# A feed-forward stage behind a recurrent attention stage: transfers put in another order at the hand-over, next input tiles loaded one by one between weight chunks, small transfers held to another stage

## The chip, the cores and the metric

One core of one Trainium2 chip. The metric is the device time of one execution in microseconds (us). One execution with a profile gives the trace that the readings below come from.

Engines: PE is TensorE's matmuls, PEld its weight loads, DVE is VectorE, ACT is ScalarE, POOL is GpSimd, SP is SyncE. SP issues nearly all loads here, on one hardware queue. GpSimd issues the small ones, on a software queue.

## The reference, cut to what matters

```python
g = _sigmoid((x * gate_w).sum(-1, keepdims=True))
a = _A_ref(x, A_mem0, A_Wq, A_Wk, A_Wv, A_Wo, A_seg_len)     # 64 segments, one after the other
b = _gelu(x @ w_gate) * (x @ w_up) @ w_down                  # x: 2048 x 1024, F = 3584, bf16
return g * a + (1 - g) * b
```

The kernel computes `a` segment by segment for about 1670 us. Then it computes `b`, the FFN, in four blocks of 512 rows, and mixes `a` and `b` at the end of each. The change touches only the FFN and the loads in front of it.

## The kernel before

A block is a gate/up stage of 28 groups (each is 8 matmuls with a gate chunk and 8 with an up chunk, 128x512), then a w_down stage of two passes. Gate and up weights stay in SBUF after block 0. w_down does not fit: each pass streams it again in 7 chunks of 1 MB through three buffers.

```python
early = [load_xo, lambda: load_xT(0), lambda: load_w(0), lambda: load_w(1), lambda: load_w(2)]
...                                    # issued by SP in this order at the end of the last segment
def load_xT(fb):                       # the x tiles of a block: four tiles of 256 KB, one transfer of 1 MB
    op("sp", lambda e: e.dma_start(xT[...], xq_scr[TB * fb:TB * fb + TB]...), wr=[xT.r()], lane="xt")
...
for fb in range(NFB):                                  # 4 blocks
    for j in range(NJ):                                # gate/up: 28 groups
        if fb == 0 and j == sum(CH[:2]):
            last_tail()                                # output matmuls of the last 4 segments; reads xo
        ...                                            # 16 matmuls, gelu and product on ACT and DVE
        if todo and j % 3 == 2:
            mix(*todo.pop(0))                          # DVE: g*a + (1-g)*b; then GpSimd stores the tile
        if j in ((8, 16) if fb == 0 else (0, 14)):
            for tb in ...: load_a(fb * TB + tb)        # GpSimd: two loads of a, 256 KB each
    for ps in range(NPS):                              # w_down: 2 passes
        for c in range(NWD):                           # 7 chunks of 1 MB
            if ps == NPS - 1 and c == 1 and not lastb:
                load_xT(fb + 1)                        # next x tiles, 1 MB
            ...                                        # 16 matmuls; todo: mix of the pass before
            load_wd()                                  # chunk c + 3, when PE is done with chunk c
        todo += [...]                                  # 4 mixes of this pass's two tiles
```

`xo` are three tiles of 512 KB of output weights. They are used only after the seventh gate/up group.

## Time and profile before

| | |
|---|---|
| time, 4 runs | 2296.72 us median (2293.88 to 2299.78) |
| profiled run | 2290.79 us, span 2288.8 us |
| FFN: last matmul of the segments to end of span | 1673.28 to 2288.8, 615.5 us |
| one w_down chunk: 16 matmuls of 0.216 us | 3.45 us |

The page of the kernel before: busy time and share of each engine.

```profile
PE 2090.5 (91%) x36642; PEld 1103.0 (48%) x36642; DVE 913.0 (40%) x2166; ACT 604.9 (26%) x1280; POOL 616.1 (27%) x1137
```

PE is busy 91% of the span, so a change has to remove what is left of PE's idle time. The waits of PE from 1600 us to the end, kernel before. Columns: the waiting instruction and its line, what it waited for, us in total, times, longest.

```profile
PE pb L1005 <- DMA wd<-in_B_w_down_dram: 10.5, 3, 3.7
PE pb L948 <- DMA wg<-in_B_w_gate_dram: 9.5, 1, 9.5
...
PE pb L719 <- DVE GT L964: 1.8, 1, 1.8
```

L1005 are the w_down matmuls, L948 the gate/up matmuls, L719 the output matmuls of the last segments. The next lines are from the timeline of PE, kernel before. Columns: start, duration, line, output<-inputs, shapes, count, and in brackets the idle time in front and what ended it.

```profile
1672.87 0.40 PE L689 MATMUL pb<-sl,oT 128*32 128x256 bf16 x8 [0.46 <-DMA sl<-in_A_Wo_dram]
1682.81 3.57 PE L948 MATMUL pb<-xT,wg 128*128 128x512 bf16 x8 [9.53 <-DMA wg<-in_B_w_gate_dram]
1686.17 2.15 PE L948 MATMUL pb<-xT,wu 128*128 128x512 bf16 x8
...
1828.51 10.53 PE L1005 MATMUL pb<-wd,GT 128*128 128x512 bf16 x48 [3.34 <-DMA wd<-in_B_w_down_dram]
...
1977.16 12.04 PE L1005 MATMUL pb<-wd,GT 128*128 128x512 bf16 x48 [3.44 <-DMA wd<-in_B_w_down_dram]
...
2127.62 11.90 PE L1005 MATMUL pb<-wd,GT 128*128 128x512 bf16 x48 [3.75 <-DMA wd<-in_B_w_down_dram]
```

There is one wait of 9.5 us at the hand-over, and one of 3.3 to 3.8 us in each of the first three w_down stages. Eight gate matmuls take 1.89 us in a steady stretch, but 3.57 us after the hand-over. The 48 matmuls after the first stall take 10.53 us, after the second and third 12.04 and 11.90. The table of stretches tells why: its third column from the right, PEclk, is the clock that PE was granted, as a share of the full clock.

```profile
core 0: us, PE busy (x) PEld busy (x) DVE busy (x) ACT busy (x) POOL busy (x), PEclk, DMA share, GB/s
...
1977.20:1980.60 3.40, 3.40 (x9) 1.25 (x10) 0.00 (x0) 0.00 (x0) 0.00 (x0) 0.55 1.06 389
2127.60:2131.00 3.40, 3.38 (x10) 1.29 (x11) 0.00 (x0) 0.00 (x0) 0.00 (x0) 0.58 1.05 386
1828.50:1832.00 3.50, 3.49 (x17) 1.61 (x18) 0.00 (x0) 0.00 (x0) 0.00 (x0) 1.00 1.05 387
```

So a stall can cost more than its length: after two of the three the clock was near half for some 3.4 us. DMA ran at about 387 GB/s, full. What was in the queue then? SP's own timeline, kernel before (start, us, queue, line, what it issues, count):

```profile
1665.68 3.96 SPq L571 DMA_DIRECT2D xo<-in_A_Wo_dram  x3
1669.69 0.47 SPq L529 DMA_DIRECT2D xT<-xq_scr  x1
1670.20 0.51 SPq L536 DMA_DIRECT2D wg<-in_B_w_gate_dram  x1
...
1815.25 0.51 SPq L529 DMA_DIRECT2D xT<-xq_scr  x1
1818.29 145.47 SPq L548 DMA_DIRECT2D wd<-in_B_w_down_dram  x14
```

At the hand-over the three xo stand ahead of what PE needs first. In the second pass of w_down the x tiles (1 MB, 1815.25) stand ahead of the chunk issued at 1818.29, and PE starts on that chunk at 1828.51, 10.2 us later. With three buffers a chunk has the computing of two others, 6.9 us, between its issue and its use. GpSimd's timeline shows what else ran then:

```profile
1814.54 0.54 POOL L934 DMA_DIRECT2D out_dram<-osb  x1 [94.67 <-DVE osb L928]
1817.30 0.55 POOL L934 DMA_DIRECT2D out_dram<-osb  x1 [2.21 <-DVE osb L928]
1817.83 1.07 POOL L554 DMA_DIRECT2D asb<-a_scr  x2
```

That is two stores and two loads of 256 KB each, 1 MB more.

### The profile page before, as it was taken

How to read it: one execution, taken by the hardware profiler on the slowest of the kernel's cores; microseconds unless marked ns; L12 is line 12 of the kernel's file. 1: busy time of each engine (PE TensorE's matmuls, PEld its weight loads, DVE VectorE, ACT ScalarE, POOL GpSimd, SP SyncE). 2: the span in 40 equal slices, each digit the busy share in tenths (PEclk: the TensorE clock that was granted, in tenths of full speed). 3: DMA queues.
4: the chain of work that ended last, by engine and by line, in shares of the span. 5: the costliest groups of instructions: out<-in, count | busy, mean ns of one | idle time of the engine just before them, and what ended most of it. 6: DMA issues, size and time to landing. Idle time of an engine off the chain costs nothing.

```text
span 2288.8 us, 80092 instructions
## 1 busy us (share of the span) xinstructions
PE 2090.5 (91%) x36642; PEld 1103.0 (48%) x36642; DVE 913.0 (40%) x2166; ACT 604.9 (26%) x1280; POOL 616.1 (27%) x1137
## 2 busy tenths in 40 slices
PE   2589999999999999999998999998879999999999
PEld 1244555555555555555555455554434444444444
DVE  3234343344343343343343343343335255263462
ACT  1122232232322233232232322222223033031230
POOL 5233333333332433423333333433210000000000
PEclk9899999999999999999999999999999999999999
DMA  9968788788788787787887887887784620704622
GB/s 349 396 208 301 270 302 290 270 300 305 268 310 292 264 321 280 265 321 277 284 318 262 282 312 268 296 312 265 262 311 154 225 87 27 268 19 143 211 88 92
DMA packets 224224, 576.43 MB, mean 252 GB/s; under 512 B 30472, under 2 KB 43272, under 8 KB 223888
## 3 DMA queue, kind: packets, MB, share of 16 engines
q1 hardware_dynamic: 190256, 513.88, 62.8%
q0 software_dynamic: 29024, 52.01, 7.3%
q8 instruction: 287, 4.70, 0.8%
q10 hardware_dynamic: 4608, 5.44, 0.7%
q14 instruction: 49, 0.40, 0.0%
HBM read 539.71 MB, written 31.39 MB: 250 GB/s over the span
## 4 chain that ended last, share of the span: by engine, by line
PE 78%; DMA 12%; issue 4%; POOL 3%; DVE 1%; ACT 1%; SPq 0%; DVEq 0%; POOLq 0%; ACTq 0%
PE pb L677 26%; PE pb L948 17%; PE pb L689 9%; PE pb L704 7%; PE pb L1005 7%; DMA sl<-in_A_Wo_dram 4%; PE pb L589 4%; PE pb L719 3%; DMA sl<-in_A_Wv_dram 3%; PE pb L610 2%; DMA wd<-in_B_w_down_dram 1%; DMA a_scr<-a_bf 1%; PE pb L604 1%; PE pb L987 1%; PE pb L643 1%
## 5 line engine op out<-in xcount | busy, mean ns | idle before, releaser
L677 PE MATMUL pb<-sl,hT 128*32 128x512 bf16 x12288 | 749.7, 383 | 22.7 <-issue 9.7
L677 PEld LDWEIGHTS pb<-sl,hT 128*32 128x32 bf16 x12288 | 332.7, 97 | 291.1 <-issue 24.9
L689 PE MATMUL pb<-sl,oT 128*32 128x256 bf16 x8192 | 282.5, 275 | 43.7 <-issue 36.4
L577 ACT ACTIVATE tok<-pb 128x512 bf16<-128x512 f32 x320 | 191.0, 597 | 428.9 <-PE pb L677 368.8
L662 POOL COPY oRc<-oT 128x128 bf16<-128x128 bf16 x128 | 97.4, 761 | 637.2 <-DVE oT L580 614.2
L689 PEld LDWEIGHTS pb<-sl,oT 128*32 128x32 bf16 x8192 | 207.7, 97 | 94.2 <-issue 47.3
L704 PE MATMUL pb<-sl,hR 128*32 128x512 bf16 x3072 | 233.8, 395 | 18.4 <-DMA sl<-in_A_Wq_dram 8.2
L948 PE MATMUL pb<-xT,wg 128*128 128x512 bf16 x896 | 213.4, 381 | 9.5 <-DMA wg<-in_B_w_gate_dram 9.5
L948 PE MATMUL pb<-xT,wu 128*128 128x512 bf16 x896 | 211.9, 379 | 0.0
L1005 PE MATMUL pb<-wd,GT 128*128 128x512 bf16 x784 | 173.3, 383 | 10.5 <-DMA wd<-in_B_w_down_dram 10.5
L580 DVE CAST oT<-pb 128x160 bf16<-128x160 f32 x256 | 71.0, 319 | 211.1 <-PE pb L653 210.7
L956 ACT ACTIVATE s<-pb 128x512 f32<-128x512 f32 x112 | 66.9, 597 | 327.1 <-PE pb L948 327.1
L934 POOL DMA_DIRECT2D out_dram<-osb x14 | 7.6, 546 | 533.0 <-DVE osb L928 533.0
L577 ACT ACTIVATE vA<-pb 128x512 bf16<-128x512 f32 x128 | 76.4, 597 | 262.6 <-PE pb L677 262.6
L948 PEld LDWEIGHTS pb<-xT,wg 128*128 128x128 bf16 x896 | 87.9, 98 | 116.1 <-issue 11.6
L580 DVE COPY kT<-pb 128x512 bf16<-128x512 bf16 x128 | 51.9, 405 | 230.1 <-PE pb L589 92.2
L948 PEld LDWEIGHTS pb<-xT,wu 128*128 128x128 bf16 x896 | 87.8, 98 | 106.2 <-issue 0.8
L589 PE MATMUL pb<-ident,tok 128*128 128x128 bf16 x1280 | 127.8, 222 | 12.0 <-ACT tok L577 3.9
L957 DVE SCALAR_TENSOR_TENSOR tp<-s,pb 128x512 f32<-128x512 f32 x112 | 76.9, 686 | 153.9 <-ACT s L956 153.6
L589 PEld LDWEIGHTS pb<-ident,tok 128*128 128x128 bf16 x1280 | 72.9, 98 | 123.4 <-ACT tok L577 92.9
L1005 PEld LDWEIGHTS pb<-wd,GT 128*128 128x128 bf16 x784 | 77.2, 99 | 106.0 <-DMA wd<-in_B_w_down_dram 12.0
L615 DVE TENSOR_REDUCE st<-pb 128x8 f32<-128x320 f32 x128 | 62.9, 491 | 146.1 <-PE pb L610 146.1
(80 smaller groups left out, 2056.8 us busy)
## 6 DMA issues: line engine op xcount, KB each, us to landing
sl<-in_A_Wv_dram SPq DMA_DIRECT2D x394, 512.0 KB, 8.8
sl<-in_A_Wo_dram SPq DMA_DIRECT2D x205, 512.0 KB, 6.0
sl<-in_A_Wk_dram SPq DMA_DIRECT2D x142, 512.0 KB, 5.6
wd<-in_B_w_down_dram SPq DMA_DIRECT2D x49, 1024.0 KB, 5.3
sl<-in_A_Wq_dram SPq DMA_DIRECT2D x79, 512.0 KB, 7.2
qk_scr<-stg POOLq DMA_DIRECT2D x64, 128.0 KB, 6.0
qkr<-qk_scr POOLq DMA_DIRECT2D x128, 64.0 KB, 2.3
wl<-in_B_w_down_dram SPq DMA_DIRECT2D x7, 1024.0 KB, 7.8
```

Of the source, the lines that this page charges most:

```text
L577: op("act", lambda e: e.activation(o, i, ACTF.Copy), rd=rd, wr=wr)
L580: op("dve", lambda e: e.tensor_copy(o, i), rd=rd, wr=wr)
L589: ins = e.transpose(PBV[TT][:, j * 128:(j + 1) * 128], tok[:, j * 128:(j + 1) * 128], ident[:, :])
L662: op("pool", lambda e: e.tensor_copy(oRc[:, u, :, :].rearrange("p c x -> p x c"), oT[:, :, :, 32:40].rearrange("p g j c -> p (g j) c")), r ...
L677: ins = e.matmul(PB[bk][32 * g:32 * g + 32, :], lhsT=h[:, i, :], rhs=w[:, g * 512:(g + 1) * 512], start=(p % 8 == 0), stop=(p % 8 == 7))
L689: ins = e.matmul(PB[XO][32 * g:32 * g + 32, 0:256], lhsT=oT[:, gp_, 2 * jj + hh, 0:32], rhs=w[:, c:c + 256], start=(r == 0 and p % 8 == 0 ...
L704: ins = e.matmul(PB[b][32 * g:32 * g + 32, :], lhsT=h[:, k[2], :], rhs=w[:, g * 512:(g + 1) * 512], start=(n == 0), stop=(n == 7))
L719: ins = e.matmul(PB[b][32 * g:32 * g + 32, 0:256], lhsT=t[:, :, 2 * i + hh], rhs=w[:, c:c + 256], start=(ends[0] and i == 0 and hh == 0), ...
L948: ins = e.matmul(PB[bk][:, 0:FB], lhsT=w[:, kc, cc:cc + 128], rhs=xT[:, :, :, kc, :].rearrange("p t i c -> p (t i) c"), start=(kc == 0), s ...
L956: op("act", lambda e, hg=hg: e.activation(s1[:, :], hg, ACTF.Square, scale=SQ), rd=[BK(bg)], wr=[s1.r()])
L957: op("dve", lambda e, hg=hg, t=t: e.scalar_tensor_tensor(out=t[:, :], in0=s1[:, :], scalar=1.0, in1=hg, op0=ALU.add, op1=ALU.mult), rd=[BK ...
L1005: ins = e.matmul(PB[bank[2 * k + hf]][:, :], lhsT=GT[:, j, tb * 128:(tb + 1) * 128], rhs=w[:, jj, hf * 512:(hf + 1) * 512], start=(j == 0) ...
```

## The change

Three things: (1) at the hand-over, x tiles and gate/up chunks 0 and 1 are issued before xo; (2) the next x tiles are loaded one by one, between the w_down chunks 1 to 4 of the second pass; (3) the small transfers of GpSimd, the stores of the first pass and the loads of a, are held until PE has done a group of the next gate/up stage, where DMA has little to do.

```diff
-        early = [load_xo, lambda: load_xT(0), lambda: load_w(0), lambda: load_w(1), lambda: load_w(2)]
+        early = [lambda: load_xT(0), lambda: load_w(0), lambda: load_w(1), load_xo, lambda: load_w(2)]
...
-        def load_xT(fb):
+        def load_xT(fb, t0=0, n=TB):                    # n of the tiles; one lane (semaphore) per t0
...
-                    if ps == NPS - 1 and c == 1 and not lastb:
-                        load_xT(fb + 1)
+                    if ps == NPS - 1 and 1 <= c <= TB and not lastb:
+                        load_xT(fb + 1, c - 1, 1)
...
+                while held:                             # in the gate/up loop, after group j = 0
+                    put(held.pop(0), 0, D, after=[pe_j])
...
-                if j in ((8, 16) if fb == 0 else (0, 14)):
+                if j in (8, 16):
                     for tb in range(2 * (j > 8), min(TB, 2 * (j > 8) + 2)):
-                        load_a(fb * TB + tb)
+                        load_a(fb * TB + tb, [pe_j])
...
-                todo += [(fb * TB + tb, 512 * hf, 512, bank[2 * k + hf]) for k, tb in enumerate(tbs) for hf in range(2)]
+                todo += [(fb * TB + tb, 512 * hf, 512, bank[2 * k + hf], "late" if ps < NPS - 1 and not lastb else "pool")
+                         for k, tb in enumerate(tbs) for hf in range(2)]
```

More of the change, by code (lines that the diff above doesn't have):

```diff
@@ L526, in bass_gated_mix__memory_aug_recurrent_mem_tr__geglu_ffn__prompt_kernel @@
         osb = [al2(f"osb{t}", [128, D]) for t in range(2)]
-        def load_xT(fb):
-            op("sp", lambda e: e.dma_start(xT[:, :, :, :, :].rearrange("p t i k c -> p t (i k c)"),
-                                           xq_scr[TB * fb:TB * fb + TB].rearrange("t p i c -> p t (i c)")),
-               rd=[("D", "xq", T) for T in range(TB * fb, TB * fb + TB)], wr=[xT.r()], lane="xt")
+        def load_xT(fb, t0=0, n=TB):
+            tn = 4 * KC * SEG
+            op("sp", lambda e: e.dma_start(xT[:, t0:t0 + n, :, :, :].rearrange("p t i k c -> p t (i k c)"),
+                                           xq_scr[TB * fb + t0:TB * fb + t0 + n].rearrange("t p i c -> p t (i c)")),
+               rd=[("D", "xq", T) for T in range(TB * fb + t0, TB * fb + t0 + n)], wr=[xT.r(t0 * tn, (t0 + n) * tn)], lane=f"xt{t0}")
         def load_w(c):
@@ L550, in load_wd, with load_a @@
                wr=[wd[n % 3].r()], lane=f"wd{n % 3}")
-        def load_a(T):
+        def load_a(T, after=()):
             t = asb[T % 4]
@@ L555, in load_a @@
                rd=[("D", "a", s) for s in range(4 * T, 4 * T + 4)] + [("D", "ar", T, g) for g in range(4)], wr=[t.r()],
-               lane=f"al{T % 4}")
+               lane=f"al{T % 4}", after=after)
         tail = slots[home["o", 0, 0]].off
@@ L930, in mix, with put @@
                rd=[BK(b), d.r(), gal.r()], wr=[ob.r(c0, c0 + n)])
-            if eng == "pool" and c0 == 0:
+            if eng != "sp" and c0 == 0:
+                return
+            if eng == "late":
+                held.append(T)
                 return
             c1 = c0 if eng == "sp" else 0
-            op(eng, lambda e: e.dma_start(of[T * 128:(T + 1) * 128, c1:c0 + n], ob[:, c1:c0 + n]),
-               rd=[ob.r(c1, c0 + n)], wr=[("D", "out", T, c0)], lane=f"out{T % 2}" if eng == "pool" else f"oute{c0}")
+            put(T, c1, c0 + n - c1, eng)
+        def put(T, c1, n, eng="pool", after=()):
+            ob = osb[T % 2]
+            op(eng, lambda e: e.dma_start(of[T * 128:(T + 1) * 128, c1:c1 + n], ob[:, c1:c1 + n]),
+               rd=[ob.r(c1, c1 + n)], wr=[("D", "out", T, c1)], lane=f"out{T % 2}" if eng == "pool" else f"oute{c1}", after=after)
+        held = []
         todo = []
@@ L951, in f @@
                         return ins
-                    op("pe", f, rd=[w.r(), xT.r()], wr=[BK(bk)])
+                    pe_j = op("pe", f, rd=[w.r(), xT.r()], wr=[BK(bk)])
+                while held:
+                    put(held.pop(0), 0, D, after=[pe_j])
                 hg, hu = PB[bg][:, 0:FB], PB[bu][:, 0:FB]
```

## The prediction

> **What bounds the kernel now.** TensorE: on the page PE is busy 2090.5 of 2288.8 us (91%) and holds 78% of the chain of waits. The change touches only the FFN (from 1673 us). There PE computes nearly without gaps, so its idle times count. PE's waits from 1600 us show two kinds that the change aims at.
>
> 1. Hand-over: 9.5 us idle (1673.3 to 1682.8) until gate chunk 0 lands. DMA is saturated (about 380 GB/s in the slices from 1660 to 1700), so its order decides. SP issues three xo loads (512 KB each) from 1665.7, x tiles (1 MB) at 1669.7, gate chunk 0 at 1670.2, landing 12.5 us later. xo is read only at 1710.8.
>
> 2. One stall in each w_down stage but the last: 3.3, 3.4, 3.8 us, at the fifth chunk of the second pass. A chunk (1 MB) is consumed in 16 matmuls, 3.45 us; with three buffers it has 6.9 us from issue to use. Median landing is 5.3 us. There 1 MB of x tiles sits ahead in the queue, and two 256 KB stores and two 256 KB loads of a (GpSimd timeline: 1814.5 to 1818.9) share the engines: the chunk took 10.2 us. After the second and third stalls the granted clock was 0.60 and 0.58 for some 4 us. Those blocks take 150.2 and 150.3 us, against 145.1 worked out from 0.216 us a matmul (672): 5.1 and 5.2 lost. Block 0 loses 3.5 in w_down.
>
> **What the change does.** No compute is added. x tiles and gate/up chunks 0 and 1 go before xo: 1.5 MB less ahead of gate chunk 0, about 4.1 us at 385 GB/s. The instruction order shows no new wait before the x tiles. The next x tiles become four 256 KB loads, one per w_down chunk; the stores of pass 0 and the loads of a move into the next gate/up stage, where DMA is nearly idle. A step of the second pass then moves 1.25 MB per 3.45 us, about 380 GB/s, for four steps: near saturation (380 to 410), but without backlog, so a chunk should land in 5.5 to 6.5 us, inside 6.9. Nine more DMA issues on SP are hidden.
>
> The Trainium skill ("DMA: Bandwidth & Descriptors", Queues, rings and completion order) says each DMA engine takes turns between queues per packet, so GpSimd's transfers delay SP's; the 10.2 us agrees. "TensorE: Matmul & The Clock Gate", Part 1, says an idle array's clock is halved until about 3.4 us of work; 0.58 and 0.60 agree, but after the first stall the clock was 1.00.
>
> **On the critical path:** all of it, PE being what each stage waits on. Hand-over -4.1; its slow first matmuls (clock 0.50, about 1.8 us lost) stay, as about 5.4 us of idling remain. Stalls with clock loss: -3.5 -5.1 -5.2 = -13.8. Sum -17.9: about 2279 us, 0.8% faster, within 2%.
>
> **What would show it.** PE's waits: about 5.4 us on gate chunk 0, none on w_down (10.5 before). Gate/up starts 145 to 146 us apart. w_down landings in the second pass at most 6.9 us. First-pass stores after the next block's first gate/up group, loads of a after groups 8 and 16; VectorE's mix at group 2 not waiting for the held stores. The 32 segments and last block unchanged.
>
> **What would make it wrong.** A 256 KB x load still pushing a chunk past 6.9 us (stalls of 1 to 3 us remain per block); the last segment's Wo loads landing later; up chunk 1 arriving just after need (margin about 1 us); a shorter idle leaving the clock full (1.8 us more gain); segments shifting by a few us.
>
> Range 2274 to 2287. Chances: faster by over 2% 0.01, within 2% 0.98, slower 0.01.

## More of the kernel before

The executions of this program differ among themselves by over 1% (the kernel before: 2281.96 to 2309.39 us over all batches), so a difference of 2 us cannot be read from the times. It can be read from the trace, stage by stage, and most of this document does that.

## The result, and the profile after

The changed kernel takes 2277.2 us in the median (2271.78 to 2279.16, 4 runs) against 2296.72; the ratio is 0.9911, with a 95% interval of 0.9888 to 0.9934. A ratio here is the mean time of one kernel's runs over that of the other's of the same rounds, so it is not quite the ratio of the medians. In two later batches it came to 0.9905 and 0.9933. So the kernel is 15 to 22 us faster, 0.7 to 1.0%, which is within 2%. The results are correct.

The line numbers moved a little: L948 became L958, L1005 became L1017, L719 became L720. PE's waits from 1600 us, changed kernel:

```profile
PE pb L958 <- DMA wg<-in_B_w_gate_dram: 4.3, 1, 4.3
...
PE pb L1017 <- DMA wd<-in_B_w_down_dram: 2.4, 3, 1.1
...
PE pb L720 <- DVE GT L976: 1.8, 1, 1.8
```

The wait at the hand-over fell from 9.5 to 4.3 us, the waits on w_down from 10.5 to 2.4 us, but not to none. PE's timeline, changed kernel:

```profile
1675.48 0.40 PE L690 MATMUL pb<-sl,oT 128*32 128x256 bf16 x8 [0.32 <-DMA sl<-in_A_Wo_dram]
1680.20 3.57 PE L958 MATMUL pb<-xT,wg 128*128 128x512 bf16 x8 [4.31 <-DMA wg<-in_B_w_gate_dram]
1683.57 3.18 PE L958 MATMUL pb<-xT,wu 128*128 128x512 bf16 x8
...
1828.38 7.17 PE L1017 MATMUL pb<-wd,GT 128*128 128x512 bf16 x31 [1.13 <-DMA wd<-in_B_w_down_dram]
...
1977.71 3.63 PE L1017 MATMUL pb<-wd,GT 128*128 128x512 bf16 x16 [0.57 <-DMA wd<-in_B_w_down_dram]
...
2123.60 3.63 PE L1017 MATMUL pb<-wd,GT 128*128 128x512 bf16 x16 [0.68 <-DMA wd<-in_B_w_down_dram]
```

The stalls that are left come one or two chunks later than before, at the sixth or seventh chunk of the second pass. SP's timeline, changed kernel: xo now stands behind, and every x tile stands between two chunks.

```profile
1669.35 0.47 SPq L530 DMA_DIRECT2D xT<-xq_scr  x1
1669.86 0.51 SPq L537 DMA_DIRECT2D wg<-in_B_w_gate_dram  x1
...
1679.99 3.92 SPq L572 DMA_DIRECT2D xo<-in_A_Wo_dram  x3
...
1813.67 0.51 SPq L530 DMA_DIRECT2D xT<-xq_scr  x1
1816.71 0.37 SPq L549 DMA_DIRECT2D wd<-in_B_w_down_dram  x1
1817.12 0.51 SPq L530 DMA_DIRECT2D xT<-xq_scr  x1
```

GpSimd's timeline, changed kernel: in the w_down stage of block 0 nothing; the stores of its first pass come after the first group of block 1 (which begins at 1835.39), the loads of a after the ninth.

```profile
1839.30 1.08 POOL L942 DMA_DIRECT2D out_dram<-osb  x2 [90.17 <-PE pb L958]
...
1866.93 1.09 POOL L555 DMA_DIRECT2D asb<-a_scr  x2 [6.71 <-PE pb L958]
```

Where the time went can be summed from the starts of the blocks (a block runs from its first gate matmul to the next block's). us, one profile each; the two last columns are the changed kernel run again (e4_again, e11_after below):

| | before | changed | again | again |
|---|---|---|---|---|
| wait on gate chunk 0 | 9.53 | 4.31 | 3.92 | 3.52 |
| block 0 | 156.07 | 155.19 | 151.94 | 152.17 |
| block 1 | 150.16 | 145.78 | 146.18 | 146.51 |
| block 2 | 150.32 | 145.90 | 145.96 | 145.04 |
| block 3 to the end | 149.44 | 149.93 | 149.91 | 149.88 |
| FFN | 615.5 | 601.1 | 597.9 | 597.1 |

The FFN is 14.4 to 18.4 us shorter. The segments in front of it are the same code but not the same time: over the 14 profiles they end between 1666.3 and 1685.4 us. That accounts for much of the spread of the times.

### The profile page after: what moved, and what is told of

The parts are those of the page before. It is cut to its first block, busy times and chain, and to the rows that moved or that the text cites. A ratio compares the mean times of both kernels' runs of the same rounds, so it can differ in the third digit from the quotient of the medians.

```text
span 2277.0 us, 80087 instructions
## 1 busy us (share of the span) xinstructions
PE 2081.6 (91%) x36623; PEld 1103.4 (48%) x36642; DVE 914.0 (40%) x2166; ACT 605.0 (27%) x1280; POOL 618.2 (27%) x1137
## 4 chain that ended last, share of the span: by engine, by line
PE 76%; DMA 12%; POOL 5%; issue 4%; DVE 1%; ACT 1%; SPq 0%; POOLq 0%; DVEq 0%; ACTq 0%
PE pb L678 24%; PE pb L958 17%; PE pb L690 8%; PE pb L705 7%; PE pb L1017 7%; DMA sl<-in_A_Wv_dram 4%; PE pb L590 4%; PE pb L720 3%; DMA sl<-in_A_Wo_dram 3%; DMA a_scr<-a_bf 2%; PE pb L611 2%; POOL v_scr L746 1%; PE pb L605 1%; PE pb L644 1%; PE pb L999 1%
## 5 line engine op out<-in xcount | busy, mean ns | idle before, releaser
L705 PE MATMUL pb<-sl,hR 128*32 128x512 bf16 x3072 | 231.4, 392 | 17.6 <-DVE xr L435 7.3
L958 PE MATMUL pb<-xT,wg 128*128 128x512 bf16 x896 | 213.4, 381 | 4.3 <-DMA wg<-in_B_w_gate_dram 4.3
L958 PE MATMUL pb<-xT,wu 128*128 128x512 bf16 x896 | 213.0, 381 | 0.0
L1017 PE MATMUL pb<-wd,GT 128*128 128x512 bf16 x766 | 169.1, 379 | 3.4 <-DMA wd<-in_B_w_down_dram 2.4
L958 PEld LDWEIGHTS pb<-xT,wg 128*128 128x128 bf16 x896 | 87.8, 98 | 111.0 <-issue 6.4
L958 PEld LDWEIGHTS pb<-xT,wu 128*128 128x128 bf16 x896 | 88.0, 98 | 107.0 <-issue 2.2
L1017 PEld LDWEIGHTS pb<-wd,GT 128*128 128x128 bf16 x784 | 76.3, 98 | 96.1 <-DMA wd<-in_B_w_down_dram 4.8
```

The costliest lines, as they stand in the source:

```text
L705: ins = e.matmul(PB[b][32 * g:32 * g + 32, :], lhsT=h[:, k[2], :], rhs=w[:, g * 512:(g + 1) * 512], start=(n == 0), stop=(n == 7))
L958: ins = e.matmul(PB[bk][:, 0:FB], lhsT=w[:, kc, cc:cc + 128], rhs=xT[:, :, :, kc, :].rearrange("p t i c -> p (t i) c"), start=(kc == 0), s ...
L1017: ins = e.matmul(PB[bank[2 * k + hf]][:, :], lhsT=GT[:, j, tb * 128:(tb + 1) * 128], rhs=w[:, jj, hf * 512:(hf + 1) * 512], start=(j == 0) ...
```

## The experiments

Two questions were open. Which of the three parts pays? And is a late chunk late because of the bytes that compete with it, whatever they are, or because of one kind of transfer? Twelve runs were made: ten new kernels, and the changed one twice. The sums of stalls are read from one profile each; each has three w_down stages to compare.

### e1_order: the order alone

```diff
 (kernel before)
-        early = [load_xo, lambda: load_xT(0), lambda: load_w(0), lambda: load_w(1), lambda: load_w(2)]
+        early = [lambda: load_xT(0), lambda: load_w(0), lambda: load_w(1), load_xo, lambda: load_w(2)]
```

> The kernel before with only the hand-over order of the change (x tiles and gate/up chunks 0 and 1 before the three xo loads). Theory: PE's wait on gate chunk 0 is the bytes queued ahead of it, so it falls from 9.5 us to 4.3 us, as in the changed kernel, and the three w_down stalls stay at 3.3 to 3.8 us. Rival: the shorter wait in the changed kernel came from a different end of the last segment (its x tiles were issued at 1669.4 us, not earlier than before), not from the order; then the wait here is 7 us or more. Total by the theory: 4 to 5 us less than before, ratio 0.998.

Measured: ratio 0.9973 (0.9938 to 1.0009), not apart from 1. PE's waits on the two kinds of weights:

```profile
PE pb L1005 <- DMA wd<-in_B_w_down_dram: 11.2, 5, 3.7
PE pb L948 <- DMA wg<-in_B_w_gate_dram: 4.3, 1, 4.3
```

The wait on gate chunk 0 was 4.34 us, as the theory said, and the stalls stayed (2.93, 3.44 and 3.69 us at the fifth chunk). Yet the FFN took 614.2 us, only 1.3 less. Block 0 gave the rest back: 159.57 us against 156.07. In it two more waits on w_down appeared (0.41 and 0.69 us), the first up group took 2.93 us instead of 2.15, and the 48 matmuls after the stall took 12.22 us instead of 10.53, that is, the clock dropped after this stall and did not drop in the profile of before. So the order does what it should, and 3.5 us of its gain were lost in block 0, mostly to the clock, in this one execution.

### e2_split: the x tiles one by one, alone

```diff
 (kernel before; load_xT takes t0 and n as in the change)
-                    if ps == NPS - 1 and c == 1 and not lastb:
-                        load_xT(fb + 1)
+                    if ps == NPS - 1 and 1 <= c <= TB and not lastb:
+                        load_xT(fb + 1, c - 1, 1)
```

> The kernel before with only the next x tiles loaded one by one between w_down chunks. Theory (all bytes that compete with the chunk count alike): the stores and loads of GpSimd, 1 MB, still delay the chunk by about 2.6 us at 390 GB/s over a slack of 1.6 us, so about 1 to 1.5 us of stall per block remain, 3 to 4.5 us in the sum instead of 10.5. Rival A (only the 1 MB x load ahead in the same queue counts): stalls as in the changed kernel, 2.4 us in the sum. Rival B (the small transfers of GpSimd are the cause): the stalls stay near 10 us. Total by the theory: 8 to 10 us less than before, with the clock loss.

Measured: ratio 0.9985 (0.9946 to 1.0024). The waits on w_down were 6.6 us in the sum: 2.45, 1.68, and 1.44 with 1.07. That is above what any of the three had named for a middle case; it lies between the theory and rival B. The FFN took 611.4 us, 4.1 less than before, where the theory had 8 to 10. PE's timeline, block 0 of this kernel:

```profile
1840.18 12.11 PE L1006 MATMUL pb<-wd,GT 128*128 128x512 bf16 x48 [2.45 <-DMA wd<-in_B_w_down_dram]
```

### e3_held: the small transfers held, alone

```diff
 (changed kernel)
-        early = [lambda: load_xT(0), lambda: load_w(0), lambda: load_w(1), load_xo, lambda: load_w(2)]
+        early = [load_xo, lambda: load_xT(0), lambda: load_w(0), lambda: load_w(1), lambda: load_w(2)]
...
-                    if ps == NPS - 1 and 1 <= c <= TB and not lastb:
-                        load_xT(fb + 1, c - 1, 1)
+                    if ps == NPS - 1 and c == 1 and not lastb:
+                        load_xT(fb + 1)
```

> The kernel before with only the stores of the first pass and the loads of a moved into the next gate/up stage; the x tiles stay one 1 MB load in front of a chunk. Theory: the chunk is 2.6 us late over a slack of 1.6, so 1 to 1.5 us of stall per block, 3 to 4.5 us in the sum. Rival A (the x load alone counts): 3.3 to 3.8 us a block stay. Rival B (the small transfers are the cause): stalls below 1 us a block. Total by the theory: 8 to 10 us less than before.

Measured: ratio 0.994 (0.99 to 0.9979). With the x tiles still one 1 MB load in front of the chunk, the stall was 0.51, 0.51 and 0.52 us; the timeline of PE in block 1 of this kernel:

```profile
1968.39 10.53 PE L1017 MATMUL pb<-wd,GT 128*128 128x512 bf16 x48 [0.51 <-DMA wd<-in_B_w_down_dram]
```

That is rival B's number, and 1.5 us in the sum is as little as the whole change leaves. FFN 602.8 us. Blocks 0 to 2 together take 444.8 us, against 456.6 before and 446.9, 444.1 and 443.7 in three profiles of the whole change. So holding the small transfers alone brings 11.7 us there, all that the whole change brings within its own spread; loading x tile by tile adds nothing that shows. Is it then the kind of the transfer that counts, and not the bytes? The next runs say no.

### e4_again and e11_after: the changed kernel once more

> The changed kernel once more, to learn what repeats: the wait on gate chunk 0 should be 4 to 5 us again, the stalls of w_down 2 to 3 us in the sum, gate/up starts 145.8 us apart, and the start of the FFN may differ by 2 to 4 us from the profile at hand, as that is where the runs differ. Ratio to before 0.991 to 0.993.

> The changed kernel on the same chip as e8 and e9, for comparison: w_down waits 1.5 to 2.4 us in the sum, wait on gate chunk 0 3.4 to 4.3 us, 1.8 us in front of the output matmuls, FFN 598 to 601 us. In the times, e8_bank should be 4 us and e9_tiles 6 us below it, at the edge of what five rounds can show, as the segments before the FFN vary by several us.

Measured: ratios 0.9905 (0.9869 to 0.9941) and 0.9933 (0.9907 to 0.9959). The waits on gate chunk 0 were 3.92 and 3.52 us. The waits on w_down came to 1.5 us in the first and 1.1 us, in one place, in the second. Three of these four are a little below what was expected of them. The columns of the table above are these two. Block 0 was 3 us shorter than in the first profile. There the first gate and up group had taken 3.57 and 3.18 us; here 3.17 and 1.89 in e4_again. What differs is the clock, and a stall of 1.1 us in block 0.

### e6_stores: e3_held with the stores set free

```diff
 (e3_held)
-                todo += [(..., "late" if ps < NPS - 1 and not lastb else "pool")
+                todo += [(..., "pool")
```

> e3_held (loads of a and first-pass stores held, x tiles in one piece, 0.51 us of stall in each block) with the stores set free again: 512 KB of stores come back beside the x load. Theory (bytes ahead, less a slack of 1.6 us): 512 KB take 1.4 us, so each block's stall grows from 0.5 to 1.9 us. Rival (it is the kind that matters, stores or loads of one kind only): either 0.5 us as before, or 3.3 us as in the kernel before.

Measured (one run, state unknown, read for its stalls only): 1.67, 2.00 and 2.09 us at the fifth chunk, 7.0 us in the sum with two smaller ones in block 0. The theory had said 1.9. PE's timeline, blocks 1 and 2:

```profile
1973.06 12.22 PE L1017 MATMUL pb<-wd,GT 128*128 128x512 bf16 x48 [2.00 <-DMA wd<-in_B_w_down_dram]
...
2122.05 10.55 PE L1017 MATMUL pb<-wd,GT 128*128 128x512 bf16 x48 [2.09 <-DMA wd<-in_B_w_down_dram]
```

These two stalls are alike, and the 48 matmuls behind them are not. The stretches of this kernel show the clock (0.60 and 1.00, third number from the right):

```profile
1973.06:1976.50 3.44, 3.44 (x10) 1.34 (x11) 0.00 (x0) 0.00 (x0) 0.00 (x0) 0.60 1.05 387
2122.05:2125.50 3.45, 3.45 (x16) 1.57 (x17) 0.00 (x0) 0.00 (x0) 0.00 (x0) 1.00 1.05 387
```

### e6_loads: a run that does not test what it should, and e10_loads: what it was meant to be

```diff
 (e3_held; e6_loads)
-                if j in (8, 16):
+                if j in ((8, 16) if fb == 0 else (0, 14)):
...
-                        load_a(fb * TB + tb, [pe_j])
+                        load_a(fb * TB + tb)
```

> e3_held with the loads of a set free again (stores stay held): 512 KB of loads come back beside the x load. Theory: 1.9 us of stall a block, as for the stores. Rival: 0.5 us (only stores matter) or 3.3 us (only loads matter).

Measured: 1.31, 0.34 and 0.88 us. It looks like "only stores matter", but GpSimd's timeline shows its loads of a at 1843.45, behind the held stores in GpSimd's own program order:

```profile
1843.45 1.08 POOL L555 DMA_DIRECT2D asb<-a_scr  x2
```

Nothing had been set free. In the w_down stages this run is e3_held once more, so it shows how far such stalls spread by themselves: 0.34 to 1.31 us (mean 0.84), against 0.51 or 0.52 three times there. Before a result is believed, the trace must show that the edit did what it says.

```diff
 (e3_held; e10_loads)
+                if fb and j == 0:
+                    for tb in range(2):
+                        load_a(fb * TB + tb)          # ahead of the held stores
                 while held:
...
-                if j in (8, 16):
+                if j in ((8, 16) if fb == 0 else (14,)):
...
-                        load_a(fb * TB + tb, [pe_j])
+                        load_a(fb * TB + tb)
```

> The run that e6_loads was meant to be: e3_held with the first two loads of a of each block put ahead of the held stores in GpSimd's order (in e6_loads they stood behind the held stores and so were held too), so that 512 KB of loads fall beside the x load as in the kernel before. Theory (bytes): about 1.9 us of stall a block, as e6_stores had (1.7, 2.0, 2.1 at the fifth chunk). Rival (stores only): 0.3 to 1.3 us, as e3_held and e6_loads had. GpSimd's timeline has to show these loads 4 to 6 us after the second pass begins, else the run tells nothing.

Measured (one run, state unknown): the loads are in the second pass now, and the stall at the fifth chunk is 1.72, 2.46 and 2.44 us, 8.3 us in the sum with four smaller ones before it (GpSimd's and PE's timelines, block 1):

```profile
1961.78 0.54 POOL L555 DMA_DIRECT2D asb<-a_scr  x1 [76.87 <-DVE dsb L927]
1964.54 0.54 POOL L555 DMA_DIRECT2D asb<-a_scr  x1 [2.22 <-DVE dsb L927]
```

```profile
1976.19 12.22 PE L1020 MATMUL pb<-wd,GT 128*128 128x512 bf16 x47 [2.46 <-DMA wd<-in_B_w_down_dram]
```

Now the bytes can be put together. Stall at the fifth chunk, mean of the three stages, with the x tiles in one piece:

| beside the 1 MB x load | stall, us |
|---|---|
| nothing (e3_held) | 0.51 |
| 512 KB of stores (e6_stores) | 1.92 |
| 512 KB of loads (e10_loads) | 2.21 |
| both (before) | 3.51 |

512 KB add 1.4 us as stores and 1.7 us as loads, both together 3.0. Stores and loads weigh about the same, by the spread seen in e6_loads, and at the fifth chunk the effects add. (Over the whole stage they add less neatly: with the smaller waits before the fifth chunk a stage waits 2.3 us in e6_stores and 2.8 in e10_loads, against 0.5 and 3.5.) So the theory of bytes stands in the main. Rival B, which says that only the small transfers count, does not fit: in e3_held the chunk behind the x load landed 7.3 us after its issue, where most chunks take 5.0 to 5.5, so the x load delays it by some 2 us too. The mirror case, the small transfers left where they were and the x tiles taken out of the stage, was not run. What misled in e3_held is the slack, the time by which a load may be late at no cost. A chunk lands in 5.3 us in the median and has 6.9, so the first 1.6 us of delay are free. The x load uses up the slack and little more; whatever comes on top of it is stall in full. The split does not take the x tiles out of the stage, it only lets fewer of them stand in front of a given chunk. The same sum, worked out afterwards, fits e2_split better than what was expected of it: 3.0 us for the small transfers, 0.5 for one x tile in front (a quarter of 2.1), less 1.6, gives 1.9 us for the first late chunk; measured were 2.45, 1.68 and 1.44.

### e5_spread: the x tiles spread over both passes

```diff
 (changed kernel)
-                    if ps == NPS - 1 and 1 <= c <= TB and not lastb:
-                        load_xT(fb + 1, c - 1, 1)
+                    if c in (2, 4) and not lastb:
+                        load_xT(fb + 1, 2 * ps + (c == 4), 1)
```

> The changed kernel with its four x tiles spread over both w_down passes (chunks 2 and 4 of each) instead of chunks 1 to 4 of the second. Theory: the stalls that the change leaves (2.4 and 1.5 us in the sum of two profiles) are a backlog of four steps of 1.25 MB in a row; with two such steps, two chunks apart, it drains, so PE waits at most 0.5 us on w_down in the whole FFN, and gate/up starts of blocks 1 to 3 lie 145.1 to 145.4 us apart (145.8 to 146.2 before). Rival: the remaining stalls are chance in the DMA rate and stay at 1.5 to 2.4 us. Total: 1 to 2 us less than the changed kernel, too little for the times to show.

Measured: ratio 0.9929 (0.9897 to 0.9961). There is no wait on w_down left in the trace; PE's waits from 1676 us to the end are these two lines and no others:

```profile
PE pb L958 <- DMA wg<-in_B_w_gate_dram: 3.4, 1, 3.4
PE pb L720 <- DVE GT L976: 1.8, 1, 1.8
```

Blocks 1 and 2 take 145.11 and 145.04 us; 672 matmuls of 0.216 us are 145.1. FFN 595.7 us. e8_bank and e9_tiles below place the x tiles in the same way and have no such wait either: none in nine stages, where the changed kernel has such waits in three, two and one of three stages in its three profiles. So spreading the x tiles removes what the change leaves. That the cause was a backlog (a queue that grows from step to step), as the theory had it, is not shown: in blocks 1 and 2 of the changed kernel the four chunks with an x tile behind them landed in 5.4, 5.5, 5.4 and 7.4 us, and in 5.4, 5.3, 5.6 and 7.5. That is one jump of 2 us, not growth. In e5_spread a chunk of block 1 took 6.7 us too, without an x tile right behind it, and the next two took 5.9 and 5.1, all inside the 6.9 us. What makes the jump is open; the spread leaves room for it.

### e7_one_xo: one xo back in front

```diff
 (changed kernel; load_xo takes the list of tiles)
-        early = [lambda: load_xT(0), lambda: load_w(0), lambda: load_w(1), load_xo, lambda: load_w(2)]
+        early = [lambda: (load_xo(lost[:1]), load_xT(0)), lambda: load_w(0), lambda: load_w(1),
+                 lambda: load_xo(lost[1:]), lambda: load_w(2)]
```

> The changed kernel with one of the three xo loads (512 KB) back ahead of the x tiles at the hand-over. Theory: PE's wait on gate chunk 0 is the bytes queued ahead of it: 4.1 us (mean of 4.3, 4.3 and 3.9) plus 512 KB at 385 GB/s, 1.4 us, gives 5.5 us (one third of the way to 8.5 to 9.5). Rival: a fixed cost of the order (the waits of the second and third xo on PE that block SP's queue, 3 us), then one xo without such a wait costs nothing and the wait stays near 4.1 us.

Measured (one run, state unknown): 5.82 us; PE's timeline:

```profile
1681.71 3.57 PE L958 MATMUL pb<-xT,wg 128*128 128x512 bf16 x8 [5.82 <-DMA wg<-in_B_w_gate_dram]
```

Six profiles with xo behind have 4.31, 4.34, 3.92, 3.36, 4.13 and 3.52 us (mean 3.9), six with xo in front 9.53, 9.26, 8.54, 7.59, 8.53 and 8.44 (mean 8.7). Three xo cost 4.7 us, one cost 1.9. SP waits for PE before the second and third xo (3.0 us in the kernel before), not before the first, and still the first costs time. So a fixed cost of these waits, the rival, does not explain it, and the bytes do; this rests on one run.

### e8_bank and e9_tiles: can the rest be had?

The output matmuls of the last segments wait 1.8 us for VectorE, which still reads the bank of PSUM (the memory that matmuls write) that they are to fill. e8_bank gives them another bank; e9_tiles also starts the first gate group in pieces.

```diff
 (e5_spread; e8_bank, in last_tail)
-            for f in wo(1, XO, oR2, (True, False), True) + wo(0, XO, oR, (False, True), True):
+            for f in wo(1, B0, oR2, (True, False), True) + wo(0, B0, oR, (False, True), True):
...
-            act_copy(a_last[:, :], PB[XO][:, 0:256], [BK(XO)], [a_last.r()])
+            act_copy(a_last[:, :], PB[B0][:, 0:256], [BK(B0)], [a_last.r()])
```

> e5_spread with the output matmuls of the last four segments (after the seventh gate/up group of block 0) written to PSUM bank 4, which is free there, instead of bank 0, which VectorE still reads for that group. Theory: PE's 1.8 us wait on GT in front of them goes, no wait on w_down appears, and the FFN (end of the last segment's matmuls to the end of the span; 615.5 before, 601.1 and 597.9 in two profiles of the change, 595.7 in e5_spread) takes 593 to 595 us. Rival: the wait only moves to the next gate group, and the FFN stays near 596.

Measured: the wait of 1.8 us is gone and did not come back elsewhere. The output matmuls start with no bracket of idle time:

```profile
1714.39 0.45 PE L720 MATMUL pb<-xo,oR 128*32 128x256 bf16 x8
```

Block 0 takes 150.48 us and the FFN 594.6, the shortest of all profiles, 2.5 us under the changed kernel in the same batch (597.1, itself below the 598 to 601 expected); part of that is the spread x tiles of e5_spread, which it includes. The times do not show it: ratio to before 0.9929 (0.9902 to 0.9957), against 0.9933 (0.9907 to 0.9959) for the changed kernel on the same chip.

```diff
 (e8_bank; e9_tiles)
-        early = [lambda: load_xT(0), lambda: load_w(0), ...
+        early = [lambda: (load_w(0, (0,)), [load_xT(0, t, 1) for t in range(TB)]), lambda: load_w(0, (1,)), ...
...                                  # first gate group of block 0: one op per x tile, 8 matmuls of 128 columns each
+                                    ins = e.matmul(PB[bk][:, t * 128:(t + 1) * 128], lhsT=w[:, kc, 0:128],
+                                                   rhs=xT[:, t, :, kc, :], start=(t == 0 and kc == 0), stop=(kc == KC - 1),
+                                                   skip_group_check=True)
```

> e8_bank with gate chunk 0 loaded first, then the four x tiles one by one, and the first gate group computed tile by tile as they land (32 matmuls of 128 columns instead of 8 of 512). Theory (bytes ahead decide): the first matmul waits for 0.75 MB instead of 1.5 MB, so PE's wait falls from 3.4 to 4.3 us to about 2.2 us, and the FFN takes about 591 to 593 us. Rival: PE then waits the rest between the tiles or before up chunk 0, and nothing is gained beyond 0.5 us.

Measured: correct, ratio 0.9924 (0.9897 to 0.9952), FFN 595.3 us. The first wait fell to 2.08 us, but two more follow, and the clock is low over a longer stretch; PE's timeline:

```profile
1686.34 1.24 PE L966 MATMUL pb<-xT,wg 128*128 128x128 bf16 x16 [2.08 <-DMA xT<-xq_scr]
1687.73 2.11 PE L966 MATMUL pb<-xT,wg 128*128 128x128 bf16 x16 [0.15 <-DMA xT<-xq_scr]
1690.36 3.60 PE L958 MATMUL pb<-xT,wu 128*128 128x512 bf16 x8 [0.52 <-DMA wu<-in_B_w_up_dram]
```

The waits add to 2.75 us instead of 4.13 in e8_bank, but the up group after them takes 3.60 us instead of 1.94. Nothing is gained in the FFN: the rival holds, in part for another reason than it named, the clock. From 1688 to 1694 us it was 0.50, in e8_bank it was 1.00 from 1692 us on, 3.6 us after its first matmul. That the start in small pieces keeps the clock low is one profile's reading, not shown.

## Why the prediction was right

The time was right: 2279 us foretold, 2277.2 measured, range 2274 to 2287. That it came within 2 us is partly luck: four runs of the changed kernel alone lie 7.4 us apart, and two terms of the sum missed in opposite directions. Point by point:

- **Hand-over, -4.1 us.** Right in mechanism, mis-sized: the three xo cost 4.7 us in the mean of twelve profiles (5.2 between the first two). They were costed at 385 GB/s; 1.5 MB in 4.7 us is about 330 GB/s.
- **"its slow first matmuls (clock 0.50, about 1.8 us lost) stay".** Right, but the size changes from run to run: from the first gate matmul to that of the second group PE took 5.4 us before, and 6.4, 4.7 and 5.0 us in three profiles of the change, where 3.5 us would do.
- **Stalls with clock loss, -13.8 us.** Blocks 1 and 2 were to gain 5.1 and 5.2 us. They gained 4.4 and 4.4 in the first profile, 4.0 and 4.4, then 3.7 and 5.3 in the others. Block 0 was to gain 3.5: it gained 0.9 in the first profile, where the clock was low for longer and a stall of 1.1 us was left, then 4.1 and 3.9.
- **"near saturation (380 to 410), but without backlog, so a chunk should land in 5.5 to 6.5 us, inside 6.9".** This step failed. The six chunks around the second pass landed in 7.4, 6.4 and 6.5 us in the median in the three stages, and 2.4, 1.5 and 1.1 us of waits on w_down remained in three profiles. The forecast of 5.5 to 6.5 us holds for the first of these chunks and fails for the last (in blocks 1 and 2 they jump from 5.4 and 5.6 to 7.4 and 7.5 us). Four steps of 1.25 MB per 3.45 us need 380 GB/s; in block 0 the steps from 1813.3 to 1827.3 us moved 312, 368, 346 and 239, though DMA ran at 386 to 389 in the stalled stages of the kernel before. So it is not shown that 380 is too much, only that a slow step found no room; e5_spread, with half as many extra tiles in a pass and a chunk between them, has no wait at all.
- **The share of the parts.** The prediction put the x tiles ahead of the chunk and the small transfers side by side as causes. The runs weigh them: holding the small ones (e3_held) removes 9.0 of 10.5 us of waits, splitting x on top of that removes nothing that shows (1.5 us left in e3_held; 2.4, 1.5, 1.1 with the split), and the split alone leaves 6.6 us.
- **"The 32 segments and last block unchanged".** The kernel has 64 segments; that count was a slip. Block 3 to the end became 0.5 us longer (149.4 to 149.9). Every kernel with the split x loads has 149.9 (149.87 to 149.93), every kernel without it 149.4. The extra time lies after the last mix on VectorE: 3.7 us with the split, 3.2 without. The split uses three more lanes, each with a semaphore that the program waits for at its end; that this is the cause was argued, not tested.
- **VectorE and the held stores.** Right: VectorE's waits from 1676 us on show none on a store.
- **Total.** The FFN lost 14.4, 17.6 and 18.4 us in three profiles, 16.8 in the mean, against 17.9. The hand-over gave 5.2 to 6.0 us instead of 4.1, blocks 0 to 2 gave 9.7 to 12.8 instead of 13.8, and the end cost 0.5: the misses cancel in part. The times of three batches gave 15 to 22 us.

The two places of the Trainium skill held up in part. "DMA: Bandwidth & Descriptors", section Queues, rings and completion order, says that each DMA engine takes turns between the queues that have work: that GpSimd's 512 KB delay SP's chunk by 1.4 to 1.7 us, on another queue, agrees. "TensorE: Matmul & The Clock Gate", Part 1, section What's actually happening, puts the low clock after at least one idle window of about 3.4 us, and says that the window runs freely, so that runs of one kernel differ. The differing agrees (4.7 to 6.4 us for the same first groups), and so does that 3.34 us idle in the kernel before left the clock at 1.00, as they are shorter than such a window. The length does not: after 2.00 us idle in e6_stores the clock was 0.60.

## What to carry to other kernels

When a load is late by less than it seems, count first the slack that it has: the first megabyte beside it may be free and the second cost its full length, so the one that is easiest to move away altogether is the one to move, whatever its kind or queue. Spread what must stay so thin that there are pauses in which a slow step can be made up. And judge a gain of a few microseconds in the stage's own interval in the trace, several times, as neither the total nor one interval is steady enough here: the clock after a stall is partly chance.

## What the Trainium skill lacked or had wrong

- "TensorE: Matmul & The Clock Gate", Part 1: at least one idle window of about 3.4 us is named for the low clock. Idle time as short as 2.00 us was followed by a clock of 0.60 here (e6_stores), so a stall below 3.4 us is not safe; after 2.09 us in the same profile the clock was 1.00.
- "DMA: Bandwidth & Descriptors", section Bandwidth, says in one place that for transfers between HBM and SBUF the HBM side, about 358 GB/s, binds, and in another that this is a core's share when both cores of a pair load. With one core at work, stretches of 3.4 us here ran at 386 to 389 GB/s, so the first wording does not hold for a single core.
- No page was found that gives the cost of each further semaphore that a program waits for at its end; three more lanes went with 0.5 us here, cause not tested.
